# Block-sparse attention into routed experts: drawn V rows gathered one slot sooner, second products taken chunk by chunk, layout work moved behind the masks

## The chip, the cores and the metric

One core of one Trainium2 chip runs the whole program in one launch. The metric is the device time of one execution in microseconds (us). Before the change the runs shown took 679.60, 681.07 and 675.01 us, a median of 679.6 us. The execution that was profiled took 677.26 us, with a span of 675.6 us from its first to its last instruction; the 1.66 us between lie around the span.

## The reference

Two blocks, one after the other, all in float32. The first is an attention in which a block of 32 queries sees its neighbours, the first and last block of keys, and three drawn blocks:

```python
batch, n_heads, seq, head_dim = (4, 8, 768, 64)
block = 32; n_rand = 3            # sampled_blocks: 24 x 3 block numbers
mask = np.abs(blk_i - blk_j) <= 1
mask |= (blk_i == 0) | (blk_j == 0) | (blk_i == n_blocks - 1) | (blk_j == n_blocks - 1)
mask[rows of qb, keys of every kb in sampled_blocks[qb]] = True
attn = softmax(where(mask, q @ k.T / 8, -1e9)) @ v
```

Its output is laid out as 3072 tokens of 512 values. The second block sends each token to the one of 8 experts with the largest logit and weighs the result with that expert's probability:

```python
logits = x @ w_gate                       # 3072 x 8
expert_idx = argmax(logits); gate_w = softmax(logits)[expert_idx]
y = maximum(x @ w1[e], 0) @ w2[e]         # w1: 512 x 1024, w2: 1024 x 512
out = gate_w[:, None] * y
```

## The kernel before

**Stages.** After a start of some 37 us (loads, lists of drawn blocks, masks, batch 0's rows for the first and last block) the attention runs until about 312 us; from there the experts run to the end.

**Steps.** The attention is one loop over 48 steps, `steps = [(b, g, half)]`: 4 batches, in each 6 groups of queries, in each group two halves of two pairs of heads. A batch's first group, `GL`, holds the last middle block and the queries of the first and last block, and has one tile; groups 0 to 4 hold 128 queries, as two tiles (`ti` 0 and 1) of 64. I call a batch's steps 0 to 11; even steps are `half` 0, odd ones `half` 1. Step i forms the scores of its own pairs of heads and exponentiates and masks them, and it takes the second products (probabilities by values) of the pairs of step i-1. `scores` fills PSUM tiles `s`; ScalarE's exponential (L331) brings them to SBUF as `ea`; VectorE masks them (L337).

**Values.** The values that a group needs lie in `around`, two buffers that groups use in turn (`parity`). Each has five slots of 128 rows, which the three chunks (`ch`) of a second product read: chunk 0 reads slot 0 (the first and last block, and the middle), chunk 1 slots 1 and 2 (one for each tile; the lower half is the tile's own block, the upper half drawn rows), chunk 2 slots 3 and 4 (drawn rows alone). The drawn rows are gathered by indirect DMAs that GpSimd issues (`fetch_values(b, g, ti, ch)`, L484): 64 rows of 2080 bytes where its `ch` is 0 (slots 1 and 2), 128 rows where it is 1 (slots 3 and 4). I name a gather by (tile, ch): (0,0), (1,0), (0,1), (1,1). They read `v_d`, a copy of V in DRAM that `keep_v` writes a batch ahead.

**Second products.** `attend` takes the 12 products of one pair of heads (three chunks, two heads, two tiles), and is called for one pair and then the other, 24 products in all; the trace shows each as two instructions. `turn_out` transposes the finished group of step i-3 into PSUM (`xr`, L433) and has ScalarE copy it (`xo`, L435); `logits` multiplies `xo` by the gate's weights (L451), and VectorE copies the result to `lgn` (L455). `divide` divides the products by their row sums (`sums` L411, `xb` L417), and SyncE writes `xb` to `x_rows`.

**What sets the order.** Through the attention every engine's order is the order of the code. GpSimd's queue is paced by hand: `not_before(at)` is a one-element copy (L496) of something that another engine writes, so that what stands behind it in the queue waits. For a group whose first step is 2j the four gathers stand at: start of step 2j-1 behind a copy of `kr` for (0,0); behind the masks of step 2j-1 (`ea`) for (1,0); behind the division in step 2j-1 (`sums`) for (0,1); and start of step 2j behind a copy of `xk` for (1,1). They are used from step 2j+1 on. `place_keys` and `place_middle` (L524, L508, L509) place drawn and middle keys two steps ahead; `place_values` (L501, L502) the values that are not drawn. `turn` (L156, L161) transposes the next batch's Q and K in steps 2 to 9 of batches 0 to 2.

**The last batch.** There `early(here)`, called at the end of each step, prepares the experts for the tokens of the batches before: `ranks` in step 2, `count` and `layout_a` in step 3, `slots_a` in step 4, `one_hots` in 6 and 7, `tokens` and three gathers of tokens (`gather`) in 8, and from step 4 on two quarter loads of expert weights in each step (`fetch_part`, on SyncE's queue).

## Time and profile before

| what | us |
|---|---|
| runs shown | 675.01, 679.60, 681.07 |
| median of them | 679.6 |
| the profiled execution | 677.26 |
| its span | 675.6 |
| PE busy in the span | 619.0 |
| DVE, ACT, POOL busy in the span | 299.0, 219.2, 205.9 |

PE is TensorE's matmuls and PEld its weight loads; DVE is VectorE, ACT ScalarE, POOL GpSimd and SP SyncE's queue. Rows of the timeline give the start and the busy time of a merged run of equal instructions, and in brackets the idle time of the engine just ahead of them with what ended it; "issue" means that the engine waited for nothing that the profile shows. A row of the waits gives what waited, what it waited for, the total in us, how many times and the longest. PEclk is the clock that TensorE was granted, as a part of its full speed.

### The profile page before, as it was taken

The numbers are of one execution on the slowest core, as the hardware profiler recorded it, in microseconds if no ns is written. First come the engines' busy times: TensorE is split into PE (matmuls) and PEld (weight loads), VectorE is DVE, ScalarE is ACT, GpSimd is POOL, SyncE is SP. The second block draws the span as 40 slices with busy tenths as digits, with TensorE's granted clock in tenths as the row PEclk, the third lists the DMA queues.
The fourth block names the chain that finished last, engine by engine and source line by source line (L and its number), as shares of the span: only waits on it lengthen the run. The fifth ranks groups of instructions, "written<-read, shape, count | busy, mean of one in ns | idle before, by whom it ended". The sixth has DMA issues, their size and how long they took to land. (4 is left out here: it accounts for less than half of the span.)

```text
span 675.6 us, 21376 instructions
## 1 busy us (share of the span) xinstructions
PE 619.0 (92%) x8952; PEld 516.6 (76%) x8952; DVE 299.0 (44%) x966; ACT 219.2 (32%) x418; POOL 205.9 (30%) x286
## 2 busy tenths in 40 slices
PE   6788889997989897979999999999999999999995
PEld 6777779887888796969777766796769679767962
DVE  5256655575557658753690158400264022802200
ACT  2356736664566555422112011112111111111110
POOL 2146754564356534570011121102210104010210
PEclk9689989999999999789999999999999999999998
DMA  9889775979586524895798999978996699979960
GB/s 191 210 196 231 202 198 138 203 177 238 134 199 163 173 78 107 266 305 189 257 322 299 325 356 379 330 261 282 404 398 242 232 391 393 371 269 386 395 214 19
DMA packets 136249, 170.93 MB, mean 253 GB/s; under 512 B 83444, under 2 KB 83445, under 8 KB 136118
## 3 DMA queue, kind: packets, MB, share of 16 engines
q1 hardware_dynamic: 126080, 137.61, 63.4%
q0 software_dynamic: 10000, 31.59, 15.6%
q8 instruction: 80, 1.31, 0.9%
q14 instruction: 51, 0.42, 0.2%
q10 hardware_dynamic: 38, 0.00, 0.0%
HBM read 150.11 MB, written 19.33 MB: 251 GB/s over the span
## 5 line engine op out<-in xcount | busy, mean ns | idle before, releaser
L1082 PEld LDWEIGHTS hp<-around,room 128*128 128x128 f32 x1216 | 138.3, 192 | 7.7 <-issue 5.5
L1082 PE MATMUL hp<-around,room 128*128 128x128 f32 x1216 | 140.9, 276 | 1.7 <-ACT kr L1089 1.4
L331 ACT ACTIVATE ea<-s 128x768 f32<-128x768 f32 x104 | 81.2, 811 | 130.0 <-PE s L326 91.1
L484 POOL DMA_INDIRECT around<-v_rows,rows_of x88 | 102.3, 1163 | 55.4 <-DMA v_rows<-room 25.1
L1063 DVE STREAM_TRANSPOSE around<-xg 32x128 f32<-32x128 f32 x208 | 62.9, 302 | 126.6 <-PE hp L1082 97.3
L1096 PE MATMUL zp<-room,kr 128*128 128x512 f32 x256 | 112.7, 594 | 0.0
L355 PE MATMUL op<-around,ea 128*64 128x65 f32 x2112 | 91.0, 231 | 23.0 <-DMA around<-v_rows,rows_of 20.3
L355 PEld LDWEIGHTS op<-around,ea 128*64 128x64 f32 x2112 | 79.8, 143 | 32.3 <-DMA around<-v_rows,rows_of 23.2
L1096 PEld LDWEIGHTS zp<-room,kr 128*128 128x128 f32 x256 | 47.5, 190 | 54.6 <-issue 54.6
L337 DVE TENSOR_TENSOR ea<-ea,mask 128x768 f32<-128x768 f32 x80 | 73.7, 953 | 15.9 <-ACT ea L331 13.6
L1111 POOL DMA_INDIRECT out_dram<-kr,sB x14 | 14.1, 1008 | 164.9 <-ACT kr L1101 106.0
L1089 ACT ACTIVATE kr<-hp 128x512 f32<-128x512 f32 x36 | 21.5, 598 | 117.1 <-PE hp L1082 103.4
L1101 ACT ACTIVATE kr<-zp,xg 128x512 f32<-128x512 f32 x16 | 11.0, 689 | 100.4 <-PE zp L1096 100.4
L1189 DVE STREAM_TRANSPOSE ea<-ea 32x128 f32<-32x128 f32 x84 | 21.6, 285 | 31.7 <-DMA ea<-x_rows,gB 31.1
L321 PE MATMUL s<-room 64*64 64x64 f32 x736 | 25.4, 232 | 6.7 <-DVE room L161 4.7
L1111 POOL DMA_INDIRECT out_dram<-kr,sA x5 | 5.1, 1021 | 82.1 <-ACT kr L1101 69.9
L321 PE MATMUL s<-other 64*64 64x64 f32 x736 | 24.8, 235 | 3.1 <-issue 1.7
L321 PEld LDWEIGHTS s<-room 64*64 64x64 f32 x736 | 20.3, 141 | 9.3 <-issue 6.7
L326 PE MATMUL s<-other,kr 64*128 64x64 f32 x352 | 27.1, 272 | 0.0
L455 DVE COPY lgn<-xr 128x8 f32<-128x8 f32 x23 | 3.8, 166 | 51.7 <-PE xr L451 51.7
L326 PE MATMUL s<-room,kr 64*128 64x64 f32 x352 | 25.5, 260 | 0.0
L326 PEld LDWEIGHTS s<-other,kr 64*128 64x128 f32 x352 | 25.4, 201 | 0.0
(339 smaller groups left out, 889.8 us busy)
## 6 DMA issues: line engine op xcount, KB each, us to landing
room<-in_moe_w_dram SPq DMA_DIRECT2D x46, 2048.0 KB
room<-in_moe_w_dram SPq DMA_DIRECT2D x16, 512.0 KB
room<-in_k_dram SPq DMA_DIRECT2D x32, 192.0 KB
room<-in_q_dram SPq DMA_DIRECT2D x32, 192.0 KB
x_rows<-xb SPq DMA_DIRECT2D x20, 256.0 KB
v_rows<-room SPq DMA_DIRECT2D x12, 260.0 KB
v_rows<-other SPq DMA_DIRECT2D x12, 260.0 KB
room<-in_v_dram SPq DMA_DIRECT2D x16, 192.0 KB
```

The costliest lines, as they stand in the source:

```text
L321: nc.tensor.matmul(s[j * D : (j + 1) * D, hh, a : a + n], lhsT=keys(r), rhs=queries(r), start=True, stop=True)
L326: nc.tensor.matmul(s[:, hh, a : a + n], lhsT=keys(r), rhs=queries(r), start=True, stop=True)
L331: nc.scalar.activation(e, s[:, :, : 6 * D], AF.Exp, scale=scale)
L337: nc.vector.tensor_tensor(e, e, m[:, None, :].to_broadcast([P, 2, 6 * D]), op=ALU.mult)
L355: nc.tensor.matmul(op[ti * D : (ti + 1) * D, pr % 2, hh, : D + 1], lhsT=e, rhs=values[:, (2 * pr + hh) * VW : (2 * pr + hh + 1) * VW], sta ...
L484: nc.gpsimd.indirect_dma_start(out=around[p0:, par, 1 + ti + 2 * ch, :], out_offset=None, in_=v_d[b][:, :], in_offset=bass.IndirectOffsetO ...
L1063: nc.vector.transpose(xT[d, :, t], xg[t, :DM].rearrange("p (c q) -> p c q", c=DB)[:, :, d])
L1082: nc.tensor.matmul(hp[:, m, :], lhsT=st[i]["w1"][:, c, fb * P : (fb + 1) * P], rhs=st[i]["xT"][:, c, :], start=(c == 0), stop=(c == DB - 1),)
L1089: nc.scalar.activation(hT[:, g * (FB // 2) : (g + 1) * (FB // 2), :], hp[:], AF.Relu)
L1096: nc.tensor.matmul(zp[:], lhsT=st[i]["hT"][:, fb, :], rhs=st[i]["w2"][:, fb, :], start=(fb == 0), stop=(fb == FB - 1),)
L1111: ins = nc.gpsimd.indirect_dma_start(out=to[:, :], out_offset=bass.IndirectOffsetOnAxis(ap=at, axis=0), in_=rows, in_offset=None, bounds_c ...
L1189: nc.vector.transpose(xT_u[d, :, j * P + tq * 32 : j * P + (tq + 1) * 32], xg_u[t, j, :DM].rearrange("p (c q) -> p c q", c=DB)[:, :, d],)
```

## The change

Five things change, all in the attention's loop.

1. The four gathers of a two-tile group each move to an earlier place. (0,0) goes from the start of step 2j-1 to the end of step 2j-2, behind that step's division; (1,0) takes its place at the start of step 2j-1; (0,1) goes behind the masks of step 2j-1, and (1,1) behind its division. For a group `GL` the two gathers move likewise. The copies of `xk` on GpSimd go.
2. `attend` takes both pairs of heads together, chunk by chunk: chunk 0 of both pairs, then chunk 1, then chunk 2.
3. `turn_out` is called behind chunk 0 (in steps that take a `GL` group's products, behind the first pair), no longer ahead of the products. ScalarE's copy of the turned Q or K, called ahead of the products, thereby stands ahead of `xo`.
4. `early` is called behind the masks, ahead of the second products and of the division, no longer at the step's end; `slots_a` is cut in two, over steps 4 and 5. The quarter loads of weights move with it on SyncE's queue.
5. The three gathers of tokens stand at the ends of steps 8, 9 and 10, one in each.

```diff
-    def attend(b, g, pr, e):
+    def attend(units_, then=None):
+
         for ch in range(3):
-            for hh in range(2):
-                for ti in range(2):
-                    x = 2 * ch + ti
-                    product(b, g, pr, ti, hh, e[:, hh, x * D : (x + 1) * D], values_of(b, g, ti, ch), ch == 2)
+            for b, g, pr, _, e in units_:
+                for hh in range(2):
+                    for ti in range(2):
+                        x = 2 * ch + ti
+                        product(b, g, pr, ti, hh, e[:, hh, x * D : (x + 1) * D], values_of(b, g, ti, ch), ch == 2)
+            if ch == 0 and then:
+                then()
...
-        if i == 4:
-            slots_a()
+        if i in (4, 5):
+            slots_a(i - 4)
...
             tokens("A", TA, KA)
-            for i_ in range(3):
-                gather(i_)
...
-        if half == 0 and i > 0 and len(tiles_of(g)) > 1:
-            if nxt is not None:
-                not_before(xk[0:1, parity(*nxt[:2]), 0, D : D + 1])
-            fetch_values(b, g, 1, 1)
-        if half == 1 and i + 1 < len(steps):
+        two = half == 1 and i + 1 < len(steps) and len(tiles_of(steps[i + 1][1])) > 1
+        if two:
             b_, g_, _ = steps[i + 1]
-            if len(tiles_of(g_)) > 1:
-                not_before(kr[0:1, parity(b_, g_), 1, 0, NKR - 1 : NKR])
-            fetch_values(b_, g_, 0, 0)
+            not_before(kr[0:1, parity(b_, g_), 1, 0, NKR - 1 : NKR])
+            fetch_values(b_, g_, 1, 0)
...
-        if half == 1 and i + 1 < len(steps) and len(tiles_of(steps[i + 1][1])) > 1:
+        if b == B - 1:
+            early(here)
+        if half == 1 and i + 1 < len(steps):
             not_before(mine[1][4][0:1, 0, 0:1])
-            fetch_values(*steps[i + 1][:2], 1, 0)
+            fetch_values(*steps[i + 1][:2], 0, 1)
...
-        out_of = None
-        if i >= 3 and half == 1:
-            out_of = steps[i - 3][:2]
-            turn_out(*out_of)
+        out_of = steps[i - 3][:2] if i >= 3 and half == 1 else None
         if copy_turned:
             copy_turned()
-        if i > 0:
-            for b_, g_, pr, e_all, e in before:
-                if g_ == GL:
-                    attend_last(b_, pr, e_all, e)
-                else:
-                    attend(b_, g_, pr, e)
+        if i > 0 and before[0][1] != GL:
+            attend(before, (lambda: turn_out(*out_of)) if out_of else None)
+        elif i > 0:
+            for n, (b_, g_, pr, e_all, e) in enumerate(before):
+                attend_last(b_, pr, e_all, e)
+                if n == 0 and out_of:
+                    turn_out(*out_of)
...
-        if i >= 2 and half == 0 and nxt is not None:
-            fetch_ends(*nxt[:2])
-        if half == 1 and i + 1 < len(steps):
+        if half == 0 and nxt is not None:
+            if i >= 2:
+                fetch_ends(*nxt[:2])
+                b_, g_, half_ = steps[i - 1]
+                not_before(sums[0:1, b_ * NG + g_, 4 * half_ : 4 * half_ + 1])
+            fetch_values(*nxt[:2], 0, 0)
+        if two:
             b_, g_, half_ = steps[i - 1]
             not_before(sums[0:1, b_ * NG + g_, 4 * half_ : 4 * half_ + 1])
-            fetch_values(*steps[i + 1][:2], 0, 1)
+            fetch_values(*steps[i + 1][:2], 1, 1)
...
-        if b == B - 1:
-            early(here)
+        if b == B - 1 and 8 <= here < 11:
+            gather(here - 8)
```

TensorE's order in an odd step that takes a two-tile group's products, as a difference (line 355 is the second products, 433 or 437 `turn_out`, 451 or 455 the logits, 156 the turn of the next batch's Q or K):

```order
 L326 MATMUL s<-room,kr 128x64 x4
 L156 MATMUL tp<-ident,room 128x64 x12
-L433 MATMUL xr<-ident,xb 128x128 x4
-L355 MATMUL op<-around,ea 64x65 x24
-L451 MATMUL xr<-wg,xo 64x8 x8
+L355 MATMUL op<-around,ea 64x65 x8
+L437 MATMUL xr<-ident,xb 128x128 x4
+L355 MATMUL op<-around,ea 64x65 x16
+L455 MATMUL xr<-wg,xo 64x8 x8
```

The four transposes moved behind the first 8 of the 24 products, and the logits stand 16 products behind them instead of 24.

ScalarE's order in that same step, before:

```order
L331 ACTIVATE ea<-s 128x768 x2
L435 COPY xo<-xr 128x512
L161 COPY other<-tp 128x2x6x64
L501 COPY around<-room 64x1040
```

and now:

```order
L331 ACTIVATE ea<-s 128x768 x2
L161 COPY other<-tp 128x2x6x64
L439 COPY xo<-xr 128x512
L505 COPY around<-room 64x1040
```

The copy of the turned Q or K (`tp`) has passed `xo`.

GpSimd's four gathers of one two-tile group, before (the copy into `paced` ahead of each names what it waits for):

```order
L496 COPY paced<-kr 1x1
L484 DMA around<-v_rows,rows_of 64x520
L496 COPY paced<-ea 1x1
L484 DMA around<-v_rows,rows_of 64x520
L496 COPY paced<-sums 1x1
L484 DMA around<-v_rows,rows_of 128x520
L496 COPY paced<-xk 1x1
L484 DMA around<-v_rows,rows_of 128x520
```

and now, the first of them at the end of the even step before:

```order
L500 COPY paced<-sums 1x1
L488 DMA around<-v_rows,rows_of 64x520
L500 COPY paced<-kr 1x1
L488 DMA around<-v_rows,rows_of 64x520
L500 COPY paced<-ea 1x1
L488 DMA around<-v_rows,rows_of 128x520
L500 COPY paced<-sums 1x1
L488 DMA around<-v_rows,rows_of 128x520
```

The last gather, (1,1), stood behind `xk` of the group's own first step, and stands behind `sums` of the step before.

VectorE's order in step 4 of the last batch, before (`slot` and `slA` belong to `slots_a`, `xb` to the division):

```order
L337 TENSOR_TENSOR ea<-ea,mask 128x768 x2
L411 TENSOR_SCALAR sums<-op 128x4
L413 RECIPROCAL r<-sums 128x4
L417 TENSOR_TENSOR xb<-op,r 128x256
L807 SCALAR_TENSOR_TENSOR offA<-loA,cnA 128x8
L808 TENSOR_SCALAR offA<-offA 128x8
L773 TENSOR_TENSOR slot<-rA,offA 128x144
L779 TENSOR_TENSOR slot<-slot,selA 128x144
L780 TENSOR_REDUCE slA<-slot 128x18
L813 TENSOR_TENSOR leftA<-used,cnA 128x8
```

and now:

```order
L337 TENSOR_TENSOR ea<-ea,mask 128x768 x2
L817 SCALAR_TENSOR_TENSOR offA<-loA,cnA 128x8
L818 TENSOR_SCALAR offA<-offA 128x8
L777 TENSOR_TENSOR slot<-rA,offA 128x144
L783 TENSOR_TENSOR slot<-slot,selA 128x144
L784 TENSOR_REDUCE slA<-slot 128x18
L415 TENSOR_SCALAR sums<-op 128x4
L417 RECIPROCAL r<-sums 128x4
L421 TENSOR_TENSOR xb<-op,r 128x256
L523 TENSOR_LOAD from_k
```

The division moved behind the five instructions of the first half of `slots_a`; the six of its second half (from `leftA` on) moved into step 5.

More of the change, by code (lines that the diff above doesn't have):

```diff
@@ L802, in layout_a, with slots_a, slots_a_1 @@
         tile_experts("A", hi, KA)
-    def slots_a():
-        cn, r, lo, used = rt["cnA"], rt["rA"], rt["lo"], rt["used"]
+    def slots_a(part=None):
+        if part != 1:
+            slots_a_1()
+        if part != 0:
+            slots_a_2()
+    def slots_a_1():
+        cn, lo = rt["cnA"], rt["lo"]
         off = small_e("offA")
@@ L810, in slots_a, with slots_a_2 @@
         summed(sl[:], "A", off)
+    def slots_a_2():
+        cn, r, used, sl = rt["cnA"], rt["rA"], rt["used"], rt["slA"]
         left = small_e("leftA")
@@ L1344 @@
             route_tokens()
-        if b == B - 1:
-            early(here)
+        if b == B - 1 and 8 <= here < 11:
+            gather(here - 8)
         before = mine
     turn_x(0)
-    for b_, g_, pr, e_all, e in before:
-        attend(b_, g_, pr, e)
+    attend(before)
     divide(*steps[-1])
```

## The prediction

> **What bounds the kernel now.** I read the table of windows first, stage by stage. Its columns are window, length, then busy us and instructions of PE, PEld, DVE, ACT and POOL, the granted clock, the share of the DMA engines and GB/s.
>
> ```profile
> 53.00:98.00 45.00, 37.09 (x947) 34.09 (x948) 27.29 (x72) 26.51 (x51) 30.84 (x55) 0.99 0.93 222
> 98.00:168.00 70.00, 62.76 (x1710) 58.07 (x1712) 41.11 (x123) 41.43 (x80) 36.90 (x51) 0.98 0.77 183
> 168.00:234.00 66.00, 60.55 (x1655) 55.91 (x1648) 40.59 (x117) 41.72 (x80) 34.09 (x43) 1.00 0.68 171
> 234.00:316.00 82.00, 72.17 (x1650) 65.95 (x1642) 51.49 (x162) 34.73 (x66) 36.26 (x45) 0.90 0.63 194
> 316.00:420.00 104.00, 103.62 (x659) 78.00 (x657) 50.83 (x203) 15.64 (x27) 14.84 (x15) 1.00 0.86 307
> ```
>
> The experts, from 316 us, are PE's: 103.62 us busy of the first 104. The change touches nothing there, so whatever the attention gains or loses arrives at the end one for one. In the attention (the rows up to 316) PE is the busiest engine too, but it idles: 70.00 - 62.76 = 7.2 us in batch 1's window, 5.5 us in batch 2's. No other engine is near full there (DVE 41.11 and ACT 41.43 of 70). Next I asked the waits for what PE idled on, in four windows: 37 to 98, 98 to 168, 168 to 234 and 234 to 316 us. One row heads every answer:
>
> ```profile
> PE op L355 <- DMA around<-v_rows,rows_of: 8.1, 6, 2.1
> ...
> PE op L355 <- DMA around<-v_rows,rows_of: 5.2, 4, 1.7
> ...
> PE op L355 <- DMA around<-v_rows,rows_of: 4.3, 4, 1.3
> ...
> PE op L355 <- DMA around<-v_rows,rows_of: 2.8, 2, 1.9
> ```
>
> So 8.1 + 5.2 + 4.3 + 2.8 = 20.4 us of PE's idle time is second products waiting for gathered rows of V, 16 waits. The timeline around one odd step (from about 127.6 us; the two gathers ahead of it are (0,1) and (1,1) of the group whose products it takes) shows which gather it is:
>
> ```profile
> 125.10 1.13 POOL L484 DMA_INDIRECT around<-v_rows,rows_of  x1 [0.54 <-PE s L326]
> 127.38 1.52 POOL L484 DMA_INDIRECT around<-v_rows,rows_of  x1 [0.16 <-issue]
> 129.23 1.51 ACT L331 ACTIVATE ea<-s 128x768 f32<-128x768 f32 x2 [1.17 <-PE s L326]
> 130.10 0.66 PE L433 MATMUL xr<-ident,xb 128*128 128x128 f32 x4
> 130.69 0.80 PE L355 MATMUL op<-around,ea 128*64 128x65 f32 x18
> 130.85 0.59 ACT L435 COPY xo<-xr 128x512 f32<-128x512 f32 x1
> 131.33 0.81 ACT L161 COPY room<-tp 128x768 f32<-128x768 f32 x1
> 132.64 1.09 PE L355 MATMUL op<-around,ea 128*64 128x65 f32 x29 [1.16 <-DMA around<-v_rows,rows_of]
> ```
>
> PE stops after 18 of 48 instructions, that is after product 9 of 24 (two instructions each). Product 10 is chunk 2, tile 1 of the first pair: it reads slot 4, which (1,1) fills. That gather was issued at 127.38, done on POOL at 127.38 + 1.52 = 128.90, and landed about 132.6, 3.7 us later. The bound of this stage is the place of (1,1) in POOL's queue, not its transfer rate.
>
> **The gathers and the products: the main term.** (1,1) moves to the slot in which (0,1) stood, 125.10 + 1.13 = 126.23 here, 128.90 - 126.23 = 2.7 us sooner. Does landing follow issue? Two other groups, from batches 0 and 2, with POOL's row and the wait that it ended, and the longest such wait:
>
> ```profile
> 57.31 0.99 POOL L484 DMA_INDIRECT around<-v_rows,rows_of  x1 [0.16 <-issue]
> 62.31 1.09 PE L355 MATMUL op<-around,ea 128*64 128x65 f32 x29 [1.44 <-DMA around<-v_rows,rows_of]
> 227.66 1.56 POOL L484 DMA_INDIRECT around<-v_rows,rows_of  x1 [0.16 <-PE op L355]
> 232.05 1.09 PE L355 MATMUL op<-around,ea 128*64 128x65 f32 x29 [1.11 <-DMA around<-v_rows,rows_of]
> 84.55 1.09 PE L355 MATMUL op<-around,ea 128*64 128x65 f32 x29 [1.88 <-DMA around<-v_rows,rows_of]
> ```
>
> Issue end to PE's restart is 62.31 - 58.30 = 4.0 us in batch 0, where the DMA engines are 0.93 busy, and 232.05 - 229.22 = 2.8 us in batch 2, where they are 0.68. That is a delay of about 3 to 4 us after issue, whichever step it is. The chunk order adds room on the other side: the first use of slot 4 comes after 17 products instead of 9. Eighteen instructions take 0.80 us and 29 take 1.09, each with the last one's drain of some 0.2 us, so about 0.03 us apiece: 16 more are 0.5 us. Room won, 2.7 + 0.5 = 3.2 us, against the longest of these waits, 1.88 us: they all go, with 1.3 us to spare.
>
> One of the 16 does not move. At the start the gathers wait for V's copy to reach DRAM, and PE for them:
>
> ```profile
> 39.01 2.43 PE L355 MATMUL op<-around,ea 128*64 128x65 f32 x20 [2.11 <-DMA around<-v_rows,rows_of]
> ```
>
> So batches 0 to 2 give 8.1 - 2.1 + 5.2 + 4.3 = 15.5 us. Batch 3's 2.8 us stand below.
>
> What hides the moved gathers: (0,0) now stands behind `sums` of the even step; its buffer's last reader is that step's products, which `sums` follows, so it finds it free. POOL is 36.90 of 70 us busy, and the copies of `xk` that go are as many as the copies of `sums` that come: 0. At a batch's end `GL`'s (0,0) is asked for a step sooner and may meet V's copy still being written; behind it on POOL stands only `GL`'s other gather, needed two steps later: 0, at most one gather's landing, 4 us once a batch, if the two steps did not cover it.
>
> **What is late next: the logits.** They wait for `xo`, which now starts behind 8 products and behind the copy of `tp`. From the rows above with the wait taken out: PE begins its products at 130.10; 16 instructions take 0.5, the four transposes 0.59 (130.10 to 130.69), 32 more instructions 1.0: logits ready for issue at 132.2. ScalarE: exponentials until 129.23 + 1.51 = 130.74, copy of `tp` 0.81 to 131.55, `xo` 0.59 to 132.14. That fits by less than 0.1 us. The lower end is 0; the upper end is the whole copy of `tp`, 0.81 us, in each odd step that has one (4 in each of three batches), 12 x 0.81 = 9.7 us. I take 0.1 each, +1.2 us, since these rows just leave a margin. Two waits of `xr` for the exponential in batch 0 (0.59 and 0.52 us) move from ahead of the transposes to ahead of the logits: 0.
>
> **The last batch.** Here DVE sets the pace in steps 3 to 5, since the layout work comes on top of its masks. One window of 4 us shows it, DVE 3.72 us busy and PE 2.18; the rows of DVE's timeline are the first and last of the layout, of the first half of `slots_a` (with the first of the second half), and its last:
>
> ```profile
> 264.00:268.00 4.00, 2.18 (x34) 1.56 (x32) 3.72 (x13) 2.96 (x4) 1.92 (x2) 0.96 0.30 44
> ...
> 259.38 0.17 DVE L740 COPY cnA<-layA 128x16 f32<-128x16 f32 x1
> 261.87 0.16 DVE L761 CAST xeA<-xfA 1x5 int32<-1x5 f32 x1
> 265.89 0.16 DVE L807 SCALAR_TENSOR_TENSOR offA<-loA,cnA 128x8 f32<-128x8 f32 x1
> 267.28 0.16 DVE L813 TENSOR_TENSOR leftA<-used,cnA 128x8 f32<-128x8 f32 x1
> 268.81 0.18 DVE L820 SCALAR_TENSOR_TENSOR slA<-slA,far 128x18 f32<-128x18 f32 x1
> ```
>
> Layout takes 262.03 - 259.38 = 2.65 us, `slots_a` 1.39 and 1.71 us. Moving them ahead of the division adds nothing to DVE, and the masks of step 4 come where they came. But `turn_out` of step 5 needs step 4's `xb`, which now follows 1.39 us more; PE met it 0.5 us later by the new place of `turn_out`:
>
> ```profile
> 266.03 0.44 PE L433 MATMUL xr<-ident,xb 128*128 128x128 f32 x2 [1.02 <-DVE xb L417]
> 269.05 1.89 PE L355 MATMUL op<-around,ea 128*64 128x65 f32 x29 [1.85 <-DMA around<-v_rows,rows_of]
> ```
>
> That wait grows to about 1.02 + 1.39 - 0.5 = 1.9 us, +0.9, and the 1.85 us wait for (1,1) behind it goes. Ends for the batch's own waits: 0 (DVE was the bound and the gain is given back) and -2.8 us + 0.9. Since DVE is the nearer limit here, I take -1. Quarter loads of weights that pass a write of `x_rows` on SP start some 5 us sooner, and the token gathers come one a step: their users are the experts' first layer after 312 us, 0.
>
> **The clock.** TensorE's clock falls around some of these waits (rows of the table of windows):
>
> ```profile
> 96.00:100.00 4.00, 3.64 (x102) 3.62 (x106) 1.21 (x5) 0.00 (x0) 0.46 (x2) 0.63 0.38 105
> 268.00:272.00 4.00, 2.96 (x54) 2.93 (x58) 3.14 (x11) 0.80 (x4) 1.46 (x2) 0.50 0.90 306
> 272.00:276.00 4.00, 4.00 (x64) 3.76 (x62) 2.02 (x9) 0.06 (x1) 3.51 (x7) 0.50 0.96 325
> 276.00:280.00 4.00, 3.95 (x94) 3.61 (x92) 2.60 (x6) 2.27 (x5) 0.74 (x1) 0.76 0.78 188
> 300.00:304.00 4.00, 4.00 (x52) 3.77 (x48) 1.55 (x4) 1.62 (x2) 3.06 (x3) 0.50 1.04 276
> ```
>
> What a reduced clock costs is window length times the missing share. At 96 us it is 4 x 0.37 = 1.5 us, just behind the last two-tile wait of batch 0. At 268 to 280 it is 4 x (0.50 + 0.50 + 0.24) = 5.0 us, behind the two waits of step 5. At 300 to 304 it is 4 x 0.50 = 2.0 us, which I leave as it is, since the change moves little there. After other waits as long (1.88 us at 84.55) the clock stayed: whether a wait trips it is chance. I take -1.5 for the first, and for the second, where one wait goes and one grows, half, -2.5 (ends 0 and -5.0).
> The Trainium skill, "TensorE: Matmul & The Clock Gate", Part 1, has the gate fall to half after an idle window of about 3.4 us. By that rule none of these waits, 2.11 us at most, would trip it, the clock terms would be 0 and the sum 4 us smaller. The trace disagrees, 0.50 granted at 268 us behind waits of 1.02 and 1.85 us, and it decides.
>
> **The sum** against the profiled execution's 677.26 us (its span 675.6 and 1.66 around it; 2.3 us under the median of 679.6): -15.5 + 1.2 - 1.0 - 1.5 - 2.5 = -19.3, so 658 us.
>
> **Rivals.** (a) The logits become the new bound: `xo` is late by the whole copy of `tp`. Against it stands that `xo` fits in the step shown, for it that the margin is under 0.1 us. 658 - 1.2 + 9.7 = 666.5 us. (b) The moved gathers land no sooner, because the DMA engines are the limit: the 0.93 share in batch 0 speaks for it, the steady 2.8 to 4.0 us from issue to landing against it. Then only the 0.5 us of the chunk order is won, in 15 waits at most 7.5: 677.3 - 7.5 = 670 us. (c) All three slow stretches of the clock go: 5.0 - 2.5 = 2.5 more and 2.0 at 300, 658 - 4.5 = 653.5 us. (d) On the other side: the longer waits of `turn_out` behind DVE's layout work, in steps 3 to 8 of the last batch, keep TensorE at half clock to the end of the attention. PE's work there from 256 to 312 us, 72.17 x 56 / 82 = 49 us by the window's row, would take as much again, less the 5.0 + 2.0 us paid already: 677.3 - 15.5 + 1.2 - 1.5 + 42 = 703.5 us at most; it ends slower than before once more than 15.8 + 7.0, about 23 us, of that work runs at half clock. For it: 0.50 at 268 us. Against: the clock was back at 0.76 in the window from 276, with PE busy.
>
> **How the numbers follow.** My forecast (653 to 663) has 0.62, (a) or a part of it 0.16, (b) 0.06, (c) 0.12, (d) 0.04. The range 648 to 668 takes in (a) and (c) and leaves out (b), (d), the far ends of the terms, and about 2 in 10. About 1% is what a measurement of this kernel can tell from no change, which puts the border at 672.8 us. All but (d) and half of (b) lie below it with room: faster 0.92, within 1% 0.05, slower 0.03.
>
> **What would show it.** In the changed profile the waits of second products for `around` fall from 20.4 us to the 2 to 3 of the start; PE's share in batch 1 and 2 rises from about 0.9 to 0.97 or more; the experts' first matmul comes near 293 instead of 312 us. If the logits (now line 455) show waits for ScalarE of over 0.3 us a group, (a) is at work; if the waits for `around` remain, (b). DVE should still be the busiest from step 3 to step 6 of the last batch. I am wrong if the waits go and the attention's end does not move.

## The result, and the profile after

The changed kernel took 651.14 us (median of 4 runs, 650.24 to 655.41), the kernel before 677.31 us beside it (4 runs, 670.42 to 681.07). The ratio is 0.969, 95% interval 0.963 to 0.974; the ratios here leave disturbed runs out, so they are not the quotients of the medians. The forecast was 658.0 us in a range of 648 to 668; the median lies inside that range and below the 653 to 663 us that the prediction gave a chance of 0.62. The profiled execution took 650.76 us against 677.26.

The page of the changed kernel, its span, busy times and the slices of the granted clock:

```profile
span 649.0 us, 21354 instructions
PE 611.7 (94%) x8952; PEld 512.0 (79%) x8952; DVE 300.9 (46%) x966; ACT 218.1 (34%) x418; POOL 184.1 (28%) x289
...
PEclk9689999999999999699999999999999999999998
```

I cut both executions at the same five places: the first mask of each batch's group `GL` (VectorE, L341), and the experts' first matmul (`hp`, at 312.3 us before and 286.0 us after). The table of windows of the kernel before, batches 0 to 3; columns as in the prediction:

```profile
35.38:103.88 68.50, 56.84 (x1408) 52.28 (x1407) 39.41 (x109) 38.90 (x76) 42.46 (x76) 0.95 0.86 204
103.88:172.25 68.37, 60.94 (x1664) 56.13 (x1660) 40.32 (x117) 41.54 (x80) 35.27 (x43) 1.00 0.79 188
172.25:238.50 66.25, 60.80 (x1664) 56.15 (x1660) 40.78 (x118) 41.72 (x80) 34.23 (x43) 1.00 0.68 170
238.50:312.30 73.80, 64.48 (x1479) 58.67 (x1473) 48.74 (x151) 32.29 (x63) 34.98 (x43) 0.88 0.63 193
```

The same of the changed kernel, and the experts:

```profile
36.80:95.56 58.76, 54.28 (x1406) 50.21 (x1404) 39.95 (x110) 38.62 (x76) 38.76 (x75) 0.97 0.94 233
95.56:158.87 63.31, 59.55 (x1663) 55.53 (x1660) 41.05 (x118) 41.13 (x80) 26.70 (x44) 1.00 0.81 202
158.87:218.64 59.77, 58.70 (x1664) 54.85 (x1660) 41.03 (x117) 41.26 (x80) 27.20 (x44) 1.00 0.73 188
218.64:286.00 67.36, 60.35 (x1479) 55.02 (x1473) 49.18 (x151) 32.46 (x63) 31.73 (x44) 0.92 0.68 227
286.00:649.00 363.00, 349.99 (x2296) 269.61 (x2294) 116.84 (x429) 54.01 (x101) 52.12 (x53) 0.99 0.83 305
```

The batches gained 9.7, 5.1, 6.5 and 6.4 us, 27.7 in all. The start before them took 1.4 us longer, and the experts 0.3 us less (675.6 - 312.3 = 363.3 before), which leaves the 26.6 us between the spans. In the last batch VectorE stays the busiest engine beside PE, with 49.18 of 67.36 us.

For the account that the rest uses, I cut the attention into windows of 1 us and added up PE's idle time, and as the cost of the clock PE's busy time times the missing share of the granted clock. What remains is PE's work at full clock.

| attention, us | length | idle | cost of the clock | rest |
|---|---|---|---|---|
| before | 276.9 | 33.9 | 11.1 | 231.9 |
| after | 249.2 | 16.3 | 6.7 | 226.2 |
| difference | -27.7 | -17.6 | -4.4 | -5.7 |

By batch, the idle time went from 11.7, 7.4, 5.5 and 9.3 us to 4.5, 3.8, 1.1 and 7.0. PE's longest waits in the whole execution of the changed kernel:

```profile
PE s L321 <- DVE room L161: 4.6, 4, 1.1
PE op L355 <- DMA around<-v_rows,rows_of: 3.9, 4, 1.9
PE s L321 <- issue: 3.7, 5, 1.5
PE xr L437 <- DVE xb L421: 3.4, 2, 2.1
PE s L326 <- issue: 2.9, 3, 1.3
```

The first row lies before batch 0 and is nearly the same in both kernels (4.7 us before). The waits for `around` fell from 20.4 to 3.9 us. The timeline, with the one wait at the start that stays, and then a steady odd step of batch 2 with the gather (1,1) of the group whose products it takes:

```profile
40.20 2.01 PE L355 MATMUL op<-around,ea 128*64 128x65 f32 x20 [1.94 <-DMA around<-v_rows,rows_of]
...
169.23 1.11 POOL L488 DMA_INDIRECT around<-v_rows,rows_of  x1 [0.54 <-PE s L326]
...
174.92 0.54 PE L156 MATMUL tp<-ident,room 64*128 64x64 f32 x12
175.39 0.69 PE L355 MATMUL op<-around,ea 128*64 128x65 f32 x16
175.92 0.81 ACT L161 COPY other<-tp 128x768 f32<-128x768 f32 x1
176.01 0.66 PE L437 MATMUL xr<-ident,xb 128*128 128x128 f32 x4
176.59 1.16 PE L355 MATMUL op<-around,ea 128*64 128x65 f32 x32
176.76 0.58 ACT L439 COPY xo<-xr 128x512 f32<-128x512 f32 x1
177.58 0.59 PE L455 MATMUL xr<-wg,xo 128*64 128x8 f32 x16
```

The 48 instructions of the products run through with no bracket. (1,1) is done on POOL at 169.23 + 1.11 = 170.34, and the transposes (`xr`, L437), behind which its first use in chunk 2 stands, begin 5.7 us later. `xo` ends at 177.34, 0.24 us ahead of the logits that need it.

In the last batch, two waits for the division and what followed:

```profile
246.78 0.44 PE L437 MATMUL xr<-ident,xb 128*128 128x128 f32 x2 [1.32 <-DVE xb L421]
...
258.02 0.44 PE L437 MATMUL xr<-ident,xb 128*128 128x128 f32 x2 [2.12 <-DVE xb L421]
...
259.75 1.02 PE L355 MATMUL op<-around,ea 128*64 128x65 f32 x13 [0.57 <-DMA around<-v_rows,rows_of]
```

```profile
258.50:259.00 0.50, 0.50 (x18) 0.50 (x18) 0.50 (x4) 0.45 (x1) 0.50 (x1) 1.00 0.52 181
259.00:259.50 0.50, 0.18 (x6) 0.04 (x1) 0.50 (x2) 0.50 (x2) 0.34 (x2) 0.68 0.90 348
...
269.00:269.50 0.50, 0.50 (x28) 0.50 (x28) 0.43 (x3) 0.00 (x0) 0.18 (x1) 0.58 0.02 8
```

The first wait is in step 5, behind `slots_a`. The second is in step 7, where the division of step 6 now stands behind `one_hots`. Windows of half a microsecond show half clock setting in at about 259.2 us and ending at about 269.4.

### The profile page after: what moved, and what is told of

It is laid out like the page before. It is cut to its first block, busy times and chain, and to the rows that moved or that the text cites. A ratio compares the mean times of both kernels' runs of the same rounds, so it can differ in the third digit from the quotient of the medians.

```text
span 649.0 us, 21354 instructions
## 1 busy us (share of the span) xinstructions
PE 611.7 (94%) x8952; PEld 512.0 (79%) x8952; DVE 300.9 (46%) x966; ACT 218.1 (34%) x418; POOL 184.1 (28%) x289
## 3 DMA queue, kind: packets, MB, share of 16 engines
q1 hardware_dynamic: 126080, 137.61, 65.4%
## 5 line engine op out<-in xcount | busy, mean ns | idle before, releaser
L488 POOL DMA_INDIRECT around<-v_rows,rows_of x88 | 92.6, 1052 | 63.5 <-DVE xk L513 25.3
L331 ACT ACTIVATE ea<-s 128x768 f32<-128x768 f32 x104 | 79.7, 809 | 91.1 <-PE s L326 70.7
L355 PE MATMUL op<-around,ea 128*64 128x65 f32 x2112 | 87.6, 228 | 5.2 <-DMA around<-v_rows,rows_of 3.9
L355 PEld LDWEIGHTS op<-around,ea 128*64 128x64 f32 x2112 | 76.3, 140 | 13.3 <-DMA around<-v_rows,rows_of 4.5
L337 DVE TENSOR_TENSOR ea<-ea,mask 128x768 f32<-128x768 f32 x80 | 73.2, 954 | 14.8 <-ACT ea L331 14.8
L326 PEld LDWEIGHTS s<-room,kr 64*128 64x128 f32 x352 | 23.9, 190 | 1.0 <-issue 1.0
L500 POOL COPY paced<-sums 1x1 f32<-1x1 f32 x42 | 7.5, 179 | 60.1 <-DVE sums L415 55.6
```

Source lines behind the costliest of these rows:

```text
L326: nc.tensor.matmul(s[:, hh, a : a + n], lhsT=keys(r), rhs=queries(r), start=True, stop=True)
L331: nc.scalar.activation(e, s[:, :, : 6 * D], AF.Exp, scale=scale)
L337: nc.vector.tensor_tensor(e, e, m[:, None, :].to_broadcast([P, 2, 6 * D]), op=ALU.mult)
L355: nc.tensor.matmul(op[ti * D : (ti + 1) * D, pr % 2, hh, : D + 1], lhsT=e, rhs=values[:, (2 * pr + hh) * VW : (2 * pr + hh + 1) * VW], sta ...
L488: nc.gpsimd.indirect_dma_start(out=around[p0:, par, 1 + ti + 2 * ch, :], out_offset=None, in_=v_d[b][:, :], in_offset=bass.IndirectOffsetO ...
```

## The experiments

Each kernel was timed against the kernel before on its chip. The ratios are to be compared with the change's 0.969 (0.963 to 0.974). For batches I give the profiled execution's length, cut as above. The account (idle time, clock, rest) is made as above, too. Lengths and accounts are of one execution each.

| kernel | median us (runs) | ratio, 95% interval | batches 0, 1, 2, 3 |
|---|---|---|---|
| gathers alone | 663.29 (6) | 0.981, 0.975 to 0.986 | 63.2, 61.6, 59.7, 74.6 |
| chunk order alone | 669.67 (12) | 0.985, 0.980 to 0.990 | (not used) |
| (1,1) back | 665.04 (6) | 0.982, 0.977 to 0.988 | 65.4, 65.7, 67.4, 69.9 |
| pair by pair | 654.03 (6) | 0.965, 0.959 to 0.970 | 57.5, 63.7, 60.9, 69.5 |
| turn_out first | 653.03 (6) | 0.965, 0.960 to 0.969 | 62.2, 62.6, 60.0, 68.2 |
| xo first | 653.66 (6) | 0.965, 0.959 to 0.971 | 59.8, 64.8, 62.8, 68.5 |
| layout at the end | 651.02 (6) | 0.961, 0.957 to 0.965 | 60.9, 63.6, 60.1, 67.4 |
| token gathers together | 653.92 (6) | 0.968, 0.963 to 0.973 | 59.3, 63.1, 60.5, 69.9 |
| layout and token gathers back | 655.79 (7) | 0.969, 0.965 to 0.973 | 57.6, 61.2, 61.5, 68.4 |
| turn_out later | 653.08 (6) | 0.966, 0.961 to 0.971 | 57.3, 67.0, 60.8, 68.0 |
| weights slower | 648.93 (6) | 0.959, 0.954 to 0.964 | 62.7, 61.6, 60.4, 62.6 |
| both of these | 649.52 (6) | 0.960, 0.954 to 0.966 | 60.5, 62.3, 59.7, 63.9 |

### Gathers alone, and chunk order alone

The first is the kernel before with the gathers' new places and nothing else. The second is the kernel before with parts 2 and 3, the gathers where they were.

> The kernel before with the gathers' new places alone (order of the products, place of turn_out, of the layout work and of the token gathers as before). If landing follows issue by 3 to 4 us, the gathers alone free every wait of the steady steps: batches 0 to 2 (from one batch's first masks of group GL to the next's) come out as in the changed kernel, about 59, 63 and 60 us against 68.5, 68.4 and 66.3 before, and the time is 652 to 656 us, the last batch keeping its layout as before. Rival: the later use of the last chunk carries the gain; then half of the waits stay and the time is 662 us or more.

> The kernel before with the products chunk by chunk and turn_out behind chunk 0 alone (gathers, layout work and token gathers as before). If landing follows issue, each wait shrinks by the 0.5 us that the use comes later: about 10 us of waits stay and the time is about 668 us. Rival, the order of the products carries the gain: 652 to 656 us.

The gathers alone gave 14.8 us of the change's 26.2 (678.09 to 663.29; by the ratios 1.9% of 3.1%) and not nearly all. The time missed the expected 652 to 656 us and lies in the rival's range of 662 or more, and 8.9 us of waits for `around` stay. But these are the one at the start (2.9 us), 0.5 us in batch 2 and 5.6 us in batch 3. Batches 1 and 2 gained as much as in the changed kernel, so landing does follow issue there. Batch 0 came out longer than the changed kernel's, and batch 3 longer than even the kernel before (74.6 against 73.8 us). The chunk order alone, with the place of `turn_out`, gave 8.4 us, as expected; but its profile still has 15.7 us of waits for `around`, in 13 waits, where about 10 us were expected, so the waits alone do not account for its gain. I use no batch of that execution, since the clock alone costs 24.6 us in it.

The end of batch 3 with the gathers alone: POOL's queue in steps 8 and 9, and PE's wait in step 11:

```profile
271.60 0.94 POOL L484 DMA_INDIRECT around<-v_rows,rows_of  x1 [0.54 <-PE layA L950]
272.85 0.95 POOL L1002 DMA_INDIRECT xg<-x_rows,gA  x1 [0.30 <-issue]
274.10 1.49 POOL L1002 DMA_INDIRECT xg<-x_rows,gA  x1 [0.30 <-DVE kr L524]
275.89 0.94 POOL L1002 DMA_INDIRECT xg<-x_rows,gA  x1 [0.30 <-DVE ea L337]
...
277.17 0.94 POOL L484 DMA_INDIRECT around<-v_rows,rows_of  x1 [0.16 <-issue]
```

```profile
282.41 0.56 PE L355 MATMUL op<-around,ea 128*64 128x65 f32 x10
286.04 0.70 PE L355 MATMUL op<-around,ea 128*64 128x65 f32 x6 [3.07 <-DMA around<-v_rows,rows_of]
```

PE stops after 10 instructions, before product 6, which reads slot 2, filled by (1,0). (1,0) stands behind three gathers of tokens (`xg`), is done on POOL at 278.11 and lands about 286.0, 7.9 us later. The experiments behind the next one ask which of parts 2 to 5 closes this gap.

### (1,1) alone back

```diff
+        if half == 0 and i > 0 and len(tiles_of(g)) > 1:
+            if nxt is not None:
+                not_before(xk[0:1, parity(*nxt[:2]), 0, D : D + 1])
+            fetch_values(b, g, 1, 1)
...
-        if two:
...
-            fetch_values(*steps[i + 1][:2], 1, 1)
```

> The changed kernel with gather (1,1) alone back at the start of the group's own first step, behind the copy of xk; the chunk order and the other three places stay. If the place of (1,1) is what the waits hung on (my theory), they return, less the 0.5 us that the chunk order leaves: in before batches 0 to 2 had 15.5 us in 13 waits, so 15.5 - 13 x 0.5 = 9 us, and 13 x 0.2 = 2.6 us less that the stops cost beside their idle time: about 660 us, and the waits of second products for around at 9 to 12 us. If the DMA engines are the limit and the landing is set by them (rival), the place matters little: 651 to 654 us.

665.04 us. One gather's place is worth 13.9 us by the medians (665.04 - 651.14) and 1.4%, some 9 us, by the ratios, in a kernel that is otherwise the changed one. The intervals of the two ratios stand apart. So the rival, that the DMA engines set the landing, falls. The waits of its whole execution:

```profile
PE op L355 <- DMA around<-v_rows,rows_of: 12.4, 11, 2.9
```

That is 8.5 us more than the changed kernel's 3.9. In the account, idle time is 24.6 us (+8.3), the clock costs 15.9 us (+9.2) and the rest is 227.8 us (+1.6). The profiled execution is one of the longest of its runs (668.49 us), so the clock's share may be a high one. The median lies 5 us above the expected 660, which left the clock out; that half clock is the difference is likely, and not shown for the median.

### Pair by pair, turn_out first, token gathers together, layout at the end

Four kernels, each the changed one with one part undone. In the first, the two outer loops of `attend` change places, with `then()` behind the first chunk of the first pair:

```diff
-        for ch in range(3):
-            for b, g, pr, _, e in units_:
+        for n, (b, g, pr, _, e) in enumerate(units_):
+            for ch in range(3):
...
-            if ch == 0 and then:
-                then()
+                if n == ch == 0 and then:
+                    then()
```

In the second, `turn_out(*out_of)` stands ahead of `attend(before)` (in steps with a `GL` group's products it stays behind the first pair). ScalarE's order stayed as in the changed kernel there (the copy of `tp` ahead of `xo`), other than the expectation says. In the third, the three `gather` calls follow `tokens` in step 8. In the fourth, `early(here)` stands at the step's end.

> The changed kernel with the second products pair by pair again (all three chunks of one pair of heads, then of the other; turn_out behind the first chunk of the first pair); the places of the gathers, of the layout and of the token gathers stay as changed. The run with the gathers alone was 12 us over the changed kernel, in batch 0 (4.4 us) and batch 3 (7.2 us). If it is the chunk order that batches 0 and 3 need (theory, a), since the landing there is slower and tile 1's drawn rows are wanted at products 6 and 10 of 24 instead of 11 and 19, this comes out the same: 658 to 664 us, batch 3 at 72 us or more, waits for around there of 3 us or more. If it is the token gathers and the layout work in their new places (rival, b), 651 to 655 us and batch 3 at 67 to 69 us.

> The changed kernel with turn_out ahead of the second products again (as before the change), the chunk order and the places of the gathers kept; the copy of tp then stands behind xo on ScalarE again. If the move of turn_out behind chunk 0 is worth nothing by itself in batches 0 to 2 (my theory: the gain is the gathers'), 650 to 654 us, the difference being the last batch's waits for xb, which come 0.3 us sooner in the step and so grow by 0.3 us each (two of them, 3.4 us before). If the transposes wait there for the exponential or the division and the products cannot cover it (rival: part 3 carries a part of the gain), each of some 20 steps shows a wait of xr of 0.2 to 0.6 us: 655 to 662 us.

> The changed kernel with the three gathers of tokens together in step 8 of the last batch, behind the lists of tokens, as before the change. If they hold up the value gathers behind them on GpSimd's queue (theory from the run that moved the gathers alone, whose last batch was 7.2 us longer than the changed kernel's, with 5.6 us of waits for around there), the waits for around in the last batch grow from 1.8 us to 4 us or more in steps 9 to 11, and the time goes to 654 to 658 us. If part 5 costs and wins nothing (my prediction), 649 to 653 us, and the last batch stays at about 67.4 us.

> The changed kernel with the layout work (and the quarter loads of weights) back at the end of the step, in the last batch; everything else as changed. If the layout's new place neither wins nor loses, since VectorE has the same work: 649 to 653 us, with the waits of turn_out for the division (3.4 us) smaller and the masks later. If it is what made the last batch 6.4 us shorter: 656 us or more. If delaying the division costs its 3.4 us: 647 to 648 us.

All four intervals overlap that of the change, each about 0.5% wide on either side. As far as these tell, no part from 2 to 5 is needed alone. For the chunk order this was nearly the rival's outcome: batch 3 is at 69.5 us, against 74.6 with the gathers alone and 67 to 69 in the rival, and the median (654.03) within the rival's range. With `turn_out` first, 653.03 us lies in the range of the theory, though batch 3 has three waits for the division (`xb`) of 5.6 us in all, more than the two of 0.3 us more each that were expected. For the token gathers, 653.92 us lies between the two ranges; batch 3 grew by 2.5 us in the profile, but the waits for `around` in it were 1.2 us and not the 4 us expected; 1.8 us of it is the clock (6.7 us instead of 5.0).

The layout's place swaps one wait for another. With it at the end, PE's waits in batch 3:

```profile
PE op L355 <- DMA around<-v_rows,rows_of: 3.5, 5, 1.5
PE op L355 <- DVE ea L337: 3.3, 4, 1.8
```

No wait for the division is left, and second products wait 3.3 us for masks that stand behind the layout work, in place of the changed kernel's 3.4 us for `xb`. Batch 3 is 67.4 us with either. The clock costs 1.7 us in it with the layout at the end and 5.0 in the changed kernel, so the equal lengths are in part chance.

### Layout and token gathers both back

> The changed kernel with parts 4 and 5 both undone: the layout work at the step's end and the three token gathers together in step 8, as before the change; places of the value gathers, chunk order and turn_out stay as changed. Each of the two undone alone made no difference that can be told, and so did the product order; the run with the gathers alone, in which all of them are undone, was 12 us over the changed kernel. Theory: 4 and 5 stand in for one another. With both undone the token gathers are issued some 5 us later in step 8 and right ahead of the last group's value gathers, which then land 7 to 8 us after issue on busy DMA engines, behind them: a wait for around of 2.5 to 3.5 us near the end of batch 3, half clock behind it, batch 3 at 71 to 75 us, in all 655 to 659 us. Rival: the chunk order or the place of turn_out covers it as well (slot 2 is wanted ten instructions later than in the run with the gathers alone): batch 3 at 67 to 69 us and 650 to 653 us.

It undoes parts 4 and 5 together. The ratio is the changed kernel's, batch 3 took 68.4 us, and its waits for `around` are 1.3 us in all, so the gap that the theory forecast is not in this profile. But the profiled execution, at 649.01 us, is the fastest of the seven, and the median, 655.79 us, lies in the theory's range of 655 to 659: the theory is not borne out, and the times alone do not rule it out. One thing this profile does show: (1,0) stands behind the same three gathers of tokens as with the gathers alone, is done on POOL at 272.80, and the products that read slot 2 ran without a stop from about 278.6 us. It had landed after at most 5.8 us, not 7.9, so that queue order by itself does not make the gap. What makes batch 3 of the gathers alone 7 us longer is not settled. That kernel has neither 2, 3, 4 nor 5, every kernel tried with at least two of them is without the gap, and no run undid 2 or 3 together with 4 and 5.

### xo first

`turn_out` and the copy of `tp` change places on ScalarE, so that `xo` never stands behind that copy.

> The changed kernel with ScalarE's copy of xo ahead of its copy of the turned Q or K again. If the logits had become the bound by 0.1 us in each of 12 steps: 1 us shorter, 650 us; if the copy of tp behind xo makes the next step's scores wait for its PSUM tile: 1 to 3 us longer. I expect 650 to 652 us, no difference that can be told, since the changed profile shows no wait of the logits for ScalarE.

653.66 us, with runs from 649.63 to 658.15. The median lies above the expected 650 to 652, but no difference from the change can be told.

### turn_out later, weights slower, and both

What is left in the changed kernel's last batch? The first takes groups 0 to 2 a step later there:

```diff
         out_of = steps[i - 3][:2] if i >= 3 and half == 1 else None
+        if b == B - 1 and 4 <= here < 11:
+            out_of = steps[i - 4][:2] if half == 0 and here >= 6 else None
```

The second spreads the quarter loads of weights:

```diff
-        for n in range(2 * (i - 4), 2 * (i - 3)):
-            if 0 <= n < 16:
+        for n in [i - 4] + (list(range(8, 16)) if i == 11 else []):
+            if n >= 0:
```

The third has both edits.

> The changed kernel with turn_out and the logits of groups 0 to 2 of the last batch one step later, in steps 6, 8 and 10 instead of 5, 7 and 9, so that the division, which stands behind the layout work on VectorE, has a step more. If the 3.4 us of waits of xr for xb (1.32 and 2.12 us in the changed kernel) and the half clock behind them are what the layout work now costs (theory), these waits go: 646 to 649 us. If VectorE is the bound there and the gain is given back at the next wait for masks (rival, as the run with the layout at the step's end suggested), 650 to 653 us.

> The changed kernel with the quarter loads of expert weights one a step (those of the first layer in steps 4 to 11) and the eight of the second layer in step 11, no longer two a step. In the changed kernel's last batch the DMA engines are 0.8 to 1.03 busy from 244 us on. If that is what makes the gathers land late there (theory), the waits for around in batch 3 go from 1.8 us to under 0.5 and half clock behind them is rarer: 647 to 650 us. If the waits for the division (3.4 us) are what is left (rival), 650 to 653 us; if the second layer's weights come late for the experts, their stage grows from 363.0 us and the time is above 653 us.

> Both: turn_out and the logits of groups 0 to 2 of the last batch one step later, and the quarter loads of weights one a step with the second layer's in step 11. The first alone took the 3.4 us of waits for the division away and had 3.7 us of waits for around in their place. If the two waits hide one another (theory), both together win what neither does: batch 3 at 62 to 64 us, 644 to 648 us. If VectorE's layout work or the clock is the bound there (rival), 650 to 653 us.

With `turn_out` later, 653.08 us is at the rival's upper end. The waits for `xb` are gone from batch 3, and the waits for `around` there have grown from 1.8 us:

```profile
PE op L355 <- DMA around<-v_rows,rows_of: 3.7, 4, 1.9
```

Batch 3 took 68.0 us: given back, by these waits and by the clock (6.8 us instead of 5.0). With the weights slower, batch 3 fell by 4.8 us to 62.64, its idle time from 7.0 to 3.7 us. The windows of batch 3 and of the experts, and the waits in batch 3:

```profile
219.86:282.50 62.64, 59.00 (x1477) 53.88 (x1472) 48.74 (x151) 32.46 (x63) 32.83 (x44) 0.95 0.57 182
282.50:647.50 365.00, 351.73 (x2298) 270.95 (x2294) 116.81 (x429) 54.02 (x101) 52.11 (x53) 0.99 0.86 314
```

```profile
PE xr L437 <- DVE xb L421: 1.3, 1, 1.3
PE op L355 <- DMA around<-v_rows,rows_of: 1.0, 1, 1.0
```

The DMA engines are 0.57 busy there instead of 0.68. The waits for `around` fell from 1.8 to 1.0 us, not under the 0.5 expected. More came from a wait that the theory did not name, the division's second one of 2.1 us. It is missing here because half clock set in earlier, at 249.3 us: the 48 instructions of step 6's products took 2.87 us instead of 1.62, and PE came to step 7 late enough. The same wait is missing in the same way from "xo first" (2.77 us), whose loads of weights are the changed kernel's. So how much of the 4.8 us is the loads' is not shown. The experts took 365.0 us, 2.0 more; with both edits, and so the same loads, they took 363.0, so the loads do not explain it. The median, 648.93 us, is the lowest of all kernels tried and 2.2 us under the change's, but the intervals (0.954 to 0.964 and 0.963 to 0.974) still touch. Both edits together give 649.52 us, above the theory's 644 to 648 and just under the rival's 650 to 653, with batch 3 at 63.9 us: no more than the second alone.

## Why the prediction was right, point by point

**The gathers.** The main term named the right cause: the place of (1,1) in POOL's queue. The waits for `around` fell to 3.9 us, 1.94 of them the one at the start that the prediction left and 1.8 in the last batch. Putting (1,1) back gave about half of the gain away. The chunk order's 0.5 us, which the prediction counted into the room, was not needed beside the earlier gathers ("pair by pair"); with the gathers in their old places, the chunk order and the place of `turn_out` together are worth 8.4 us.

**Where the size was off.** The prediction took -15.5 us for the waits of batches 0 to 2, with +1.2 for the logits and -1.5 for the clock: -15.8. These batches gained 21.3. Their idle time fell by 15.3 us (24.6 to 9.3), as the term said. The clock gave 1.6 (3.3 to 1.7). The remaining 4.4 us lie in the rest, PE's busy time at full clock, for which the prediction has no term. The gathers' new places alone bring it about: in batches 1 and 2 the gathers alone, whose products and transposes stand as before, took it from 121.7 to 116.9 us, the changed kernel to 118.3. The waits of second products for `around` went from 14 to 2 in batches 0 to 2, so that is up to 0.4 us a wait, an estimate (short gaps of other kinds went too). About half of that has a cause that the trace shows: one product instruction is booked with 0.22 us, while the next begins some 0.03 us behind it, so each stop books about 0.2 us more of busy time. The prediction named this drain of "some 0.2 us" when it counted instructions, and did not count it as part of what a wait costs. The other half stays open.

**The logits.** The +1.2 us did not come. No wait of the logits for ScalarE of 0.3 us or more stands in the changed trace, the margin being 0.24 us in the step shown, and "xo first" won nothing. Rival (a) is out.

**The last batch.** The prediction gave -1.0 for its own waits and -2.5 for the clock, -3.5. It gained 6.4: 2.3 of idle time, 2.8 of the clock and 1.3 of the rest. The waits for the division grew to 3.4 us as feared, more than the 1.9 us: the prediction priced `slots_a` in step 5, where the wait came to 1.32 us, and overlooked `one_hots`, which the same part of the change moves ahead of the division in step 6 and which costs the longer wait of 2.12 us in step 7. That the clock gave about the 2.5 us forecast is luck. The half clock that the prediction halved, 5.0 us of cost behind step 5, came back whole behind the division's wait at 259 us, 5.0 us again. What went is the half clock at 300 to 304 us, "which I leave as it is, since the change moves little there": PE had been busy only 1.17 us of the 3.41 before it. And the size is not the change's alone: in the other kernels whose ratio interval overlaps the change's, the clock costs between 1.7 and 8.2 us in batch 3, against 7.8 in the kernel before.

**Rivals.** (b) is out by the (1,1) experiment. (c) gives 653.5 us, the nearest to the measured time, but came true only in part: the stretches at 96 and 300 us went, that of the layout moved and stayed as long. The profiled time is 7.2 us under the forecast, mainly by the 4.4 us of the rest, the 1.2 of the logits and the 2.9 that batch 3 gained beyond its term, less the 1.4 that the start took longer; no rival named the rest. (d) did not occur: half clock ended after 10 us with PE busy.

**What would show it.** The waits for `around` came to 3.9 us, a little over the 2 to 3 forecast. PE's share rose to 0.98 in batch 2 (58.70 of 59.77), but only to 0.94 in batch 1, where 3.6 of the 3.8 us of idle time are waits for nothing that the profile shows ("issue"). The experts' first matmul came at 286.0 us, not near 293. VectorE stayed the busiest while the layout work ran, from 238 to 258 us: 18.2 of 20.0 us, PE 15.7.

**What stays open.** The gathers alone are 12 us over the change by the medians, 1.2% or some 8 us by the ratios. The 4.4 us in batch 0 may be chance: "weights slower", whose code for that batch is the changed kernel's, took 62.7 us there in its execution, and the clock costs 4.4 us of it, against 4.5 with the gathers alone and 1.7 in the changed kernel. The 7.2 us in batch 3 were not traced to a part.

## What to carry over

Where an engine stops for a gather, compare the end of its issue with the moment it landed in several groups: if that delay is steady, move the gather's place in its queue and not its size. Count a wait as its idle time plus the drain ahead of it, some 0.2 us here, an estimate. One profiled execution does not tell what the clock gained; compare it over several kernels or executions. When several parts of a change each give room against the same wait, undo them one at a time and expect little from each; and when a wait off the path is taken away in a stage with two near limits (here the division and the gathers behind the weights' loads), look which of them is late next before calling it won.

## What was not expected of the hardware

Half clock comes in stretches that are multiples of one length, and they begin on a grid. By the shares in half-microsecond windows (the last fence of the first section; 0.68 granted in the first mixed window is 0.64 of it at half clock), the stretch of the changed kernel runs from 259.18 to 269.42, 10.24 us. In the kernel before:

```profile
267.50:268.00 0.50, 0.00 (x0) 0.00 (x0) 0.47 (x2) 0.50 (x1) 0.00 (x0) 0.67 0.70 183
277.50:278.00 0.50, 0.50 (x13) 0.50 (x14) 0.24 (x1) 0.50 (x1) 0.00 (x0) 0.59 1.12 191
...
298.00:298.50 0.50, 0.07 (x3) 0.07 (x3) 0.00 (x0) 0.00 (x0) 0.00 (x0) 0.89 1.05 404
...
305.00:305.50 0.50, 0.50 (x16) 0.43 (x14) 0.00 (x0) 0.00 (x0) 0.00 (x0) 0.78 0.90 125
```

267.67 to 277.91 is 10.24 us, and 298.39 to 305.22 is 6.83 us: three times and twice 3.41 us. One such unit costs 1.7 us of work. The two begin 30.72 us apart, nine times 3.413. All fourteen profiled executions agree: laid out as windows of 3.413 us from one stretch's beginning, the 1105 windows between about 34 and 310 us show a granted clock of 0.50 (97) or of 1.00 (1008), and none a mixture. What counts is how long PE is busy within one such window, not how long one wait is. All 27 full-clock windows with PE busy for 1.71 us (half) or less were followed by half clock, 19 of the 62 with 1.72 to 2.37 us, and none of the 919 with more. Three windows show it, the one ahead of 259 us in the changed kernel, and from the kernel before the one ahead of 267.67 and the one into which the wait of 1.88 us at 84.55 runs:

```profile
255.77:259.18 3.41, 1.29 (x22) 0.86 (x20) 2.79 (x11) 0.63 (x2) 1.12 (x2) 1.00 0.83 313
...
264.26:267.67 3.41, 1.92 (x30) 1.30 (x28) 3.17 (x12) 2.44 (x4) 1.66 (x2) 1.00 0.30 32
...
83.35:86.76 3.41, 2.21 (x78) 2.12 (x78) 0.27 (x4) 1.52 (x4) 2.16 (x4) 1.00 1.13 328
```

That last wait lies across a border of the grid, 0.68 us on one side and 1.20 on the other, and no half clock follows. So what the prediction called chance, whether a wait trips the clock, is in good part where the wait falls on the grid and what else leaves PE idle beside it. Between 1.72 and 2.37 us of busy time, what decides stays open.

The Trainium skill, "TensorE: Matmul & The Clock Gate", Part 1, names windows of about 3.4 us by which the gate decides; the lengths agree with it, while the trigger does not, as the prediction found: at 259 us no single idle stretch was longer than 2.12 us, and PE was busy through most of the stretch before the clock came back. The spread between runs of one kernel (650.18 to 656.70 us for the token gathers together) is of the size of a few such units; whether it is that, no profile shows.

The gathers' landing is not fixed: 2.8 to 4.0 us after issue in the steady batches of the kernel before, and behind three gathers of tokens 7.9 us with the gathers alone (DMA share 1.03 from 280 to 284 us) but at most 5.8 us with layout and token gathers back (1.05 from 272 to 276 us). Neither the place in the queue nor the share alone tells which.
